# The sink columns of an attention kernel: four per head, turned by VectorE and gathered by DMAs, in place of eight turned by TensorE

## The chip, the cores and the metric

One core of one Trainium2 chip runs the whole kernel. The metric is device time in microseconds; the kernel before has a median of 690.72 us over three runs (690.72 to 690.74).

## The reference

Attention over a window of 128 keys and the first four keys ("sinks"), for 4 sequences of 768 positions and 8 heads of 64, and then two dense layers over all 3072 tokens:

```
scores = q k^T / 8,  kept where key < 4 or 0 <= query - key < 128
a = exp(scores - max) / (sum + 1e-9)
x = a v                       (3072 x 512, heads side by side)
out = relu(x w_in)^2 w_out    (512 -> 2048 -> 512)
```

All in float32, the weights given in float64.

## The kernel before, in words

The 3072 tokens are cut into eight chunks c of 384 (half a sequence), each with three blocks of 128 queries. For each chunk the attention runs in four steps s, one for a pair of heads; so there are 32 steps. Then come the first products (w_in, lines L778: twelve matmuls of 384 columns per piece of 128 hidden channels), the activation on ScalarE (L791, L795) and VectorE (L800, L807), which split the square into a high part gh and a low part gl, and the second products (L823: nine matmuls of 512 columns per piece). The products of chunk c cover the attention of chunk c + 1. Products go in two or three passes of rounded float32 ("fp32r": high and low parts).

One attention step: the scores of a block of 128 queries against 128 + NS + 128 columns (own and previous key block and NS sink columns: BAND = 264 with NS = 8) on TensorE (L483 in the first eight steps, "plain", with full float32; L489 with high and low parts after that); mask, scale and row maximum on VectorE (L466); exp on ScalarE (L472); sums and reciprocals on VectorE (L529, L530); scaling by 1/sum on GpSimd (L537), or on ScalarE (L535) in the plain steps. Then the probabilities P are turned, keys to partitions. In the first two chunks ("turned") TensorE transposes P (L638) and ScalarE copies to PT or PTS. From the third chunk on VectorE turns 32 x 32 blocks (L668, L672) into T, four DMAs store T in DRAM (via, L685) and one loads it as PT (L698).

The sink columns go another way. GpSimd copies those of both heads into PSK (L552) in three groups of 32 columns: a high part, a low part (L550) and the high part once more. TensorE transposes each block of PSK (L590), in all 32 steps: two 128 x 128 transposes in the first half of a sequence (its first block has no sink columns beside the window) and three in the second half. A copy takes the result from PSUM to SK (L600). The product with v (L726, two matmuls side by side on half the columns of the array) is closed by one matmul of SK with VS (L730), whose rows hold v at the sinks: high parts, high parts, low parts (L374, L379).

The order of each engine's instructions is written out by a planner (class Plan). Every step is added with an engine, or a list of engines to choose from, a cost, a rank, the cells that it reads and writes, and the PSUM banks that it takes and gives back. The planner goes through time with these costs: on each engine, of the steps that could start within 0.03 us of the first, it takes the one with the lowest rank. It knows that GpSimd and some VectorE steps ("port") hinder each other, that a change of TensorE's tiling costs something, and that a DMA takes its time and its share of the rate. The engines then run their lists strictly in order.

Of the kernel before, what the change touches and what calls it, by code (L numbers as in the profile page):

```python
# [19 lines left out]
D = 64  # L20
NS = 8
# [11 lines left out]
EPS = 1.0e-9  # L33
URGE = 0.5
# [15 lines left out]
class Plan:  # L50
# [45 lines left out]
    def order(self):  # L96
# [3 lines left out]
        while open_:  # L100
# [24 lines left out]
            if e == "PE":  # L125
                cost += 0.17 * (kind[0] != mode)
                mode = kind[0]
# [27 lines left out]
def sink_window_attention_moe(  # L155
# [25 lines left out]
    with ExitStack() as fast:  # L181
# [78 lines left out]
        SK = [sb("SK", [P, TOK], F32R, "SK_0"), sb("w22", [P, TOK], F32R, "SK_1")]  # L260
# [100 lines left out]

        def sinks(b, rank):
            rows = vs.shape[1]
            raw = lambda: sb("VR", [rows, NPAIR, P], F32, f"vs_{b}")
            lo = slice(64, 64 + 2 * NS)
# [5 lines left out]
                writes=["VR"],  # L371
# [3 lines left out]
                reads=["VR"], writes=["VS"],  # L375
# [3 lines left out]
                lambda: nc.vector.tensor_tensor(VS[lo], raw()[lo], f32(VS[lo]), op=ALU.subtract),  # L379
                reads=["VR"], writes=["VS"],  # L380
            )

        def attention(s, rank):
# [117 lines left out]
            for m, (i, heads) in enumerate(order):  # L501
# [3 lines left out]
                if plain:  # L505
                    reads, cost = [q_cell, (k_cell, 0), (k_cell, 1)], (0.44 if n > P else 0.23)
                else:
# [5 lines left out]
                    reads=reads, writes=keys, take=[("any" if early else "att", key) for key in keys],  # L513
# [27 lines left out]
            two = s % 2 if plain else 0  # L541
            psk = PSK[two]
            psk_cell = "PSK" if two == 0 else ("spare", 23)
            to = psk.rearrange("p q (t c) -> p q t c", c=32)

            def part_sinks(h, low):
                own = slice(h * NS, h * NS + NS)
                src = Pt(h)[:, i0:NQ, P:BS]
                if low:
                    nc.gpsimd.tensor_tensor(to[:, i0:NQ, 1, own], src, f32(to[:, i0:NQ, 0, own]), op=ALU.subtract)  # L550
                else:
                    nc.gpsimd.tensor_copy(  # L552
                        to[:, i0:NQ, 0:3:2, own], src.unsqueeze(2).broadcast_to([P, NQ - i0, 2, NS])
                    )

            groups = ((0, 1),) if plain else ((0,), (1,))
            for heads in groups:
# [6 lines left out]
                for h in heads:  # L564
                    for i in range(NQ):
# [3 lines left out]
                            [pool, ("ACT", 0.38 if n > P else 0.28, "", SC_ACT)] if plain else [pool, pool], r - URGE,  # L569
# [6 lines left out]
                        reads=done, writes=[(psk_cell, h)] + ([] if two == 0 else [psk_cell]),  # L576
# [6 lines left out]
            sk = SK[two]  # L583
            sk_cell = "SK" if two == 0 else ("spare", 22)
            nsq = (NQ - i0) * P
            key = ("sk", s)

            def turn_sinks():
                for i in range(i0, NQ):
                    nc.tensor.transpose(bank(key)[:, (i - i0) * P : (i - i0 + 1) * P], f32(psk[:, i]), ident)  # L590

            r = rank(0.95)
            add(
                ("PE", 0.11 * (NQ - i0), 0), r, turn_sinks,
                reads=[(psk_cell, h, *x) for h in range(2) for x in ((), (1,))] + ([] if two == 0 else [psk_cell]),
                writes=[key], take=[("any" if early else "att", key)],
            )
# [4 lines left out]
            on_act, on_dve = ("ACT", 0.36 if nsq == TOK else 0.3, "", 0.0), ("DVE", 0.48 if nsq == TOK else 0.36, "", CP_DVE)  # L602
            add(
# [556 lines left out]
```

## Time and profile before

| | |
|---|---|
| median of three runs | 690.72 us |
| the profiled execution | 688.96 us |
| its span, first to last instruction | 686.9 us |
| mean granted clock of TensorE | 0.991 |
| TensorE busy | 667.4 us (97%) |
| VectorE, ScalarE, GpSimd busy | 459.1, 375.0, 215.2 us |
| DMA queue of the kernel | 103.98 MB, 49.7% of 16 engines |

Lines such as L778 are lines of the kernel before. In a row, PE is TensorE, PEld its weight loads, DVE VectorE, ACT ScalarE, POOL GpSimd, SPq the queue of SyncE, which issues all DMAs. A row of a timeline gives the start, the time from the first start to the last end of the merged instructions, engine, line, operation, output and inputs, how many, and in brackets the idle time ahead and what ended it. Matmuls overlap, so the duration of one is longer than the time to the start of the next.

### The profile page before, as it was taken

To read this page: it belongs to the slowest core of one execution; us is meant where nothing else is said; L and a number is where in the kernel's file an instruction comes from. 1 tells how busy PE (TensorE), PEld (TensorE's weight loads), DVE (VectorE), ACT (ScalarE), POOL (GpSimd) and SP (SyncE) were. 2 spreads that over 40 slices of the span, in tenths; PEclk is the share of its full clock that TensorE was granted. 3 is DMA by queue.
4 is the path that set the end of the run, shared out by engine and by line. 5 is a ranking of instruction groups with operands and counts; after the bars stand their busy time and mean duration, and the time that the engine had idled before them with its cause. 6 is when DMAs were issued, how large, how long until landed. Compare 5 with 4: busy or idle time off the path is not lost.

```text
span 686.9 us, 11380 instructions
## 1 busy us (share of the span) xinstructions
PE 667.4 (97%) x3722; PEld 581.1 (85%) x3722; DVE 459.1 (67%) x1194; ACT 375.0 (55%) x1073; POOL 215.2 (31%) x377
## 2 busy tenths in 40 slices
PE   4999989999999999999999999999999999999996
PEld 3667879998888888888888898888898888899985
DVE  7599999967987655676677766666776764242222
ACT  6798734355464434456666656666666565442221
POOL 4455433534544513232244323223332322000000
PEclk9799999999999999999999999999999999999999
DMA  7746455215777532466556666555557754310001
GB/s 244 220 163 203 168 192 183 84 52 157 223 245 227 154 106 93 134 207 193 155 148 184 211 188 201 170 167 174 145 169 213 223 160 114 116 51 12 0 1 51
DMA packets 58178, 104.78 MB, mean 153 GB/s; under 512 B 6208, under 2 KB 34624, under 8 KB 58112
## 3 DMA queue, kind: packets, MB, share of 16 engines
q1 hardware_dynamic: 58112, 103.98, 49.7%
q8 instruction: 31, 0.51, 0.3%
q14 instruction: 35, 0.29, 0.1%
HBM read 79.58 MB, written 24.38 MB: 151 GB/s over the span
## 4 chain that ended last, share of the span: by engine, by line
PE 90%; DVE 6%; ACT 1%; issue 1%; DMA 1%; SPq 0%; POOL 0%; DVEq 0%
PE bank L823 37%; PE bank L778 37%; PE bank L726 6%; PE bank L489 5%; PE bank L730 1%; DVE f L310 1%; PE bank L590 1%; PE bank L483 1%; DVE P L466 1%; PE bank L638 1%; DVE f L317 1%; DVE f L303 1%; DMA kn<-in_k_dram 1%; ACT w L323 0%; DVE w L327 0%
## 5 line engine op out<-in xcount | busy, mean ns | idle before, releaser
L778 PE MATMUL bank<-x,w 128*128 128x384 f32 x1536 | 303.1, 339 | 0.7 <-DVE gl L807 0.7
L778 PEld LDWEIGHTS bank<-x,w 128*128 128x128 f32 x1536 | 267.0, 188 | 9.5 <-issue 1.4
L823 PE MATMUL bank<-w,gh 128*128 128x512 f32 x768 | 242.7, 397 | 2.1 <-ACT ob L864 2.1
L823 PEld LDWEIGHTS bank<-w,gh 128*128 128x128 f32 x768 | 137.5, 188 | 21.4 <-ACT ob L864 2.4
L823 PE MATMUL bank<-w,gl 128*128 128x512 f32 x384 | 151.4, 394 | 0.0
L446 POOL TENSOR_TENSOR KS<-kn,KS 128x408 fp32r<-128x408 f32 (+1 forms) x48 | 64.9, 1352 | 225.1 <-DVE KS L441 164.2
L791 ACT ACTIVATE r<-bank 128x384 f32<-128x384 f32 x128 | 62.7, 490 | 129.3 <-PE bank L778 128.2
L472 ACT ACTIVATE P<-P,nbs 128x264 f32<-128x264 f32 (+1 forms) x192 | 94.4, 492 | 66.5 <-DVE nbs L466 65.7
L800 DVE TENSOR_TENSOR bank<-bank,r 128x384 f32<-128x384 f32 x128 | 72.1, 563 | 83.4 <-ACT r L791 83.1
L537 POOL TENSOR_SCALAR P<-P,small 128x128 f32<-128x128 f32 (+1 forms) x168 | 88.5, 543 | 71.1 <-DVE small L530 48.9
L823 PEld LDWEIGHTS bank<-w,gl 128*128 128x128 f32 x384 | 72.1, 188 | 16.6
L466 DVE CUSTOM_DVE_ANT_0 P<-bank,maskA 128x264 f32<-128x264 f32 x128 | 53.4, 426 | 45.1 <-PE bank L489 43.6
L807 DVE TENSOR_TENSOR gl<-bank,gh 128x384 fp32r<-128x384 f32 x128 | 70.9, 554 | 17.4 <-ACT gh L795 11.8
L795 ACT ACTIVATE gh<-r 128x384 fp32r<-128x384 f32 x128 | 66.7, 521 | 4.7 <-PE bank L823 2.2
L668 DVE STREAM_TRANSPOSE T<-P 128x384 f32<-128x384 f32 x96 | 45.2, 495 | 22.6 <-POOL P L537 21.7
L489 PEld LDWEIGHTS bank<-KS,QS 128*128 128x128 f32 x288 | 51.6, 188 | 6.2 <-DVE nbs L466 0.4
L489 PE MATMUL bank<-KS,QS 128*128 128x264 f32 (+1 forms) x288 | 55.4, 279 | 0.0
L742 ACT CAST x<-bank 128x384 fp32r<-128x384 f32 x32 | 15.3, 478 | 52.6 <-PE bank L730 52.4
L327 POOL TENSOR_TENSOR w<-f,w 128x512 fp32r<-128x512 f32 x19 | 27.1, 1430 | 51.4 <-ACT w L323 51.4
L726 PE MATMUL bank<-PT,vn 128*64 128x256 f32 (+1 forms) x392 | 40.6, 347 | 0.0
L726 PEld LDWEIGHTS bank<-PT,vn 128*64 128x64 f32 x392 | 25.7, 139 | 15.5 <-issue 6.7
L529 DVE TENSOR_TENSOR small<-small,eps 128x3 f32<-128x3 f32 (+1 forms) x56 | 34.5, 616 | 3.3 <-ACT P L472 2.7
(90 smaller groups left out, 575.5 us busy)
## 6 DMA issues: line engine op xcount, KB each, us to landing
raw<-in_moe_w_dram SPq DMA_DIRECT2D x32, 512.0 KB, 3.7
half<-in_moe_w_dram SPq DMA_DIRECT2D x64, 256.0 KB, 3.6
via<-T SPq DMA_DIRECT2D x48, 192.0 KB, 3.7
PT<-via SPq DMA_DIRECT2D x12, 768.0 KB, 4.4
via<-T SPq DMA_DIRECT2D x48, 160.0 KB, 4.2
PT<-via SPq DMA_DIRECT2D x12, 640.0 KB, 4.7
kn<-in_k_dram SPq DMA_DIRECT2D x24, 272.0 KB, 4.4
qn<-in_q_dram SPq DMA_DIRECT2D x32, 192.0 KB, 3.6
```

The lines of the kernel that those rows point to most:

```text
L446: lambda h=h: nc.gpsimd.tensor_tensor(KS(h)[:, 1, 0:nk], kn()[:, h, 0:nk], f32(KS(h)[:, 0, 0:nk]), op=ALU.subtract),
L466: nc.vector.tensor_tensor_reduce(Pt(h)[:, i, o : o + n], ps_[:, 0:n], mask[:, 0:n], -SCALE, BIG, ALU.add, ALU.min, nb)
L472: nc.scalar.activation(Pt(h)[:, i, o : o + n], Pt(h)[:, i, o : o + n], AF.Exp, bias=nb, scale=-1.0, accum_out=sm[:, h, i : i + 1],)
L489: nc.tensor.matmul(bank(key)[:, 0:n], QS(h)[:, cols], flat[:, a, c0 : c0 + n], start=(a == 0), stop=(a == 1),)
L537: {"POOL": nc.gpsimd, "DVE": nc.vector}[engine].tensor_scalar(a, a, rs[:, h, i : i + 1], 1.0, op0=ALU.mult, op1=ALU.mult)
L726: nc.tensor.matmul(xo[h * D : h * D + D, qs[0] * P : qs[0] * P + len(qs) * P], vn[:, kk, h, :], rhs(), start=(n == 0), stop=False, skip_gr ...
L778: nc.tensor.matmul(bank(key)[:, 0:TOK], wi[fc][:, i, cc * P : (cc + 1) * P], xt[:, cc, :], start=(cc == 0 and j == 0), stop=(cc == NCC - 1 ...
L791: lambda key=key, r=r: nc.scalar.activation(r(), bank(key)[:, 0:TOK], AF.Relu),
L795: ("ACT", 0.41), n - 9, lambda gh=gh, r=r: nc.scalar.activation(gh(), r(), AF.Square),
L800: lambda key=key, r=r: nc.vector.tensor_tensor(bank(key)[:, 0:TOK], bank(key)[:, 0:TOK], r(), op=ALU.mult),
L807: lambda key=key, gh=gh, gl=gl: nc.vector.tensor_tensor(gl(), bank(key)[:, 0:TOK], f32(gh()), op=ALU.subtract),
L823: nc.tensor.matmul(bank(okey), gt()[:, ts_], wo[f][:, i, :], start=(f == f0 and j == 0), stop=(f == f1 - 1 and j == 2),)
```

## The change

NS becomes 4, so a score block has 260 columns. The rest of the change has three parts.

The turning of the sinks. In the steps from the third chunk on, PSK is 32 columns wide: 4 columns of two heads, three times (high, low, high), 24 in use. VectorE turns each 32 x 32 block (L633) into SKT, four DMAs gather the four strips of 32 partitions (L639) into a tile that shares its place with the raw rows of v at the sinks, and a copy (L610) on ScalarE or VectorE brings them into 32 partitions of SK. The closing product (L776) reads SK with a pattern (block, strip, 32 columns), and VS has its low parts in rows 16 to 23 (made with a column "third" of 0 and -1). The first eight steps keep the transposes on TensorE (L616), from a wide PSK that has two buffers.

The engines for scalings. In the eight plain steps VectorE may scale too (L556), beside GpSimd and ScalarE.

The planner. A GpSimd step and a "port" step of VectorE hinder each other for half their cost (SHARE) instead of all; a step that could start up to 0.15 us later (HOLD) but has a rank lower by more than 8 goes first; a tiling change costs 0.2 instead of 0.17 and is also counted at the end of a step; the scores of a later step are put in order only when the tile for P is free (CLAIM).

```
-NS = 8
+NS = 4
+SHARE = 0.5
+HOLD = 0.15
+SC_DVE = 0.3
+CLAIM = (True, False)
...
+                urgent = [x for x in able if x[0] <= first + HOLD and x[1] < a[1] - 8]
+                if urgent:
+                    a = min(urgent, key=lambda a: a[1:3])
...
-                    port[e] = t + cost
+                    port[e] = t + SHARE * cost
...
-        PSK = [sb("PSK", [P, NQ, P], F32R, "PSK_0"), sb("w23", [P, NQ, P], F32R, "PSK_1")]
-        for t in (VS, *PSK):
+        PSK = [wp.tile([P, NQ, 32], F32R, name=f"PSK{i}") for i in range(2)]
+        SKT = wp.tile([P, NQ, 32], F32, name="SKT")
+        SK = [sb("SK", [P, 4, NQ, 32], F32R, "SK_0"), sb("w22", [P, 4, NQ, 32], F32R, "SK_1")]
+        PSKW = sb("w23", [P, 2, NQ, P], F32R, "PSK_wide")
+        for t in (VS, PSKW, *PSK, *SK):
             nc.gpsimd.memset(f32(t), 0.0)
...
-                    reads=reads, writes=keys, take=[("any" if early else "att", key) for key in keys],
+                    reads=reads + [P_cell(h) for h in heads] * (CLAIM[plain] and i > 0),
+                    writes=keys + [P_cell(h) for h in heads] * (CLAIM[plain] and i == 0), take=[...],
...
-                            [pool, ("ACT", 0.38 if n > P else 0.28, "", SC_ACT)] if plain else [pool, pool], r - URGE,
+                            [
+                                pool, ("ACT", 0.38 if n > P else 0.28, "", SC_ACT),
+                                ("DVE", 0.25 if n > P else 0.18, "port", SC_DVE),
+                            ] if plain else [pool, pool], r - URGE,
...
+            else:
+                add(
+                    ("DVE", 0.18), rank(1.0) - URGE,
+                    lambda: nc.vector.transpose(SKT[:, i0:NQ], f32(psk[:, i0:NQ])), reads=own_sinks, writes=["SKT"],
+                )
+                rows_ = lambda: sb("VR", [P, 4, NQ, 32], F32, f"sk_{s}")
+                def gather(x):
+                    nc.sync.dma_start(
+                        out=rows_()[0:32, x, i0:NQ].rearrange("p i b -> p (i b)"),
+                        in_=SKT[32 * x : 32 * x + 32, i0:NQ].rearrange("p i b -> p (i b)"),
+                    )
+                for x in range(4):
+                    add(
+                        ("SP", 0.42, 2.5, 13), rank(0.85), lambda x=x: gather(x), reads=["SKT"], writes=[("VR", x)],
+                    )
+                add(
+                    [("ACT", 0.4), ("DVE", 0.35, "port", CP_DVE)], rank(0.8) - URGE,
+                    lambda e: copy(e, sk[0:32, :, i0:NQ], rows_()[0:32, :, i0:NQ]),
+                    reads=VR, writes=[sk_cell],
+                )
...
-                    xo[:, i0 * P : TOK], VS[:, p], sk[:, 0:nsq], start=False, stop=True, skip_group_check=True
+                    xo[:, i0 * P : TOK], VS[:, p], sk[:, :, i0:NQ].rearrange("p r i b -> p i r b"), start=False, stop=True, skip_group_check=True
```

How the order moves, at three places. First TensorE in the third quarter of the program, in a step of a second half: the product with v closes, and the transposes of the next step's sinks follow. Before:

```order
L726 MATMUL bank_67<-PT,vn_136 64x256 x4
L726 MATMUL bank_67<-PT,vn_136 64x128 x4
L730 MATMUL bank_67<-SK_132,VS 128x384
L778 MATMUL bank_71<-x_140,w_996 128x384 x2
L778 MATMUL bank_71<-x_141,w_996 128x384
L590 MATMUL bank_69<-ident,PSK_127 128x128 x3
L823 MATMUL bank_74<-w_971,gh_597 128x512 x2
L823 MATMUL bank_74<-w_971,gl_605 128x512
```

And after:

```order
L772 MATMUL bank_69<-PT,vn_146 64x256 x4
L772 MATMUL bank_69<-PT,vn_146 64x128 x4
L776 MATMUL bank_69<-SK_130,VS 128x384
L824 MATMUL bank_70<-x_150,w_987 128x384 x2
L824 MATMUL bank_70<-x_151,w_987 128x384
L869 MATMUL bank_74<-w_959,gh_597 128x512 x2
L869 MATMUL bank_74<-w_959,gl_606 128x512
```

The three transposes between first and second products are gone, and nothing stands in their place; the same holds for two or three of them in 24 steps.

Second VectorE in such a step. Before, the copy of the transposes of the sinks (SK) stands right behind the turning of P (T), between the product and the subtraction of the activation:

```order
L668 STREAM_TRANSPOSE T_3764<-P_1_3746 128x2x4x32
L672 STREAM_TRANSPOSE T_3764<-P_1_3746 128x4x32
L747 TENSOR_TENSOR x_139<-bank_68,x_138 128x384
L800 TENSOR_TENSOR bank_71<-bank_71,r_567 128x384
L864 COPY ob_0_0_3872<-bank_74 128x512
L807 TENSOR_TENSOR gl_590<-bank_71,gh_578 128x384
L600 CAST SK_132<-bank_67 128x384
```

And after, where SKT is VectorE's turning of the sinks and sk the tile that the four DMAs fill:

```order
L633 STREAM_TRANSPOSE SKT<-PSK_128 128x96
L718 STREAM_TRANSPOSE T_3822<-P_1_3801 128x4x32
L793 TENSOR_TENSOR x_149<-bank_68,x_148 128x384
L846 TENSOR_TENSOR bank_70<-bank_70,r_560 128x384
L853 TENSOR_TENSOR gl_586<-bank_70,gh_579 128x384
L910 COPY ob_0_0_3934<-bank_72 128x512
L910 COPY ob_0_2_3943<-bank_73 128x512
...
L610 CAST SK_130<-sk_3908 32x384
```

The copy of the sinks now stands one step of the products behind the turning, and ahead of the next product (L846); the two reductions of scores ahead of it are left out. On SP the four gathers stand behind a load of v and ahead of most of the stores of T in such a step.

Third the first scalings of the program, on GpSimd. Before (P_0_171 and P_1_173 are the two heads of the first step):

```order
L537 TENSOR_SCALAR P_0_171<-P_0_171,small 128x128
L537 TENSOR_SCALAR P_0_171<-P_0_171,small 128x264 x2
L537 TENSOR_SCALAR P_1_173<-P_1_173,small 128x128
L537 TENSOR_SCALAR P_1_173<-P_1_173,small 128x264 x2
L552 CAST PSK_127<-P_0_171 128x4x8
```

And after:

```order
L556 TENSOR_SCALAR P_0_181<-P_0_181,small 128x128
L556 TENSOR_SCALAR P_0_181<-P_0_181,small 128x260
L556 TENSOR_SCALAR P_1_187<-P_1_187,small 128x260
L572 CAST PSK_wide<-P_0_181 128x2x2x4
L572 CAST PSK_wide<-P_1_187 128x2x2x4
```

The other three of the six now stand on VectorE, between its reductions of the scores. In all, VectorE has 16 scalings in the first eight steps, ScalarE 7 instead of 24, and GpSimd's number is one higher.

More of the change, by code (lines that the diff above doesn't have):

```diff
@@ L378, in sinks @@
                 ("DVE", 0.62, "port"), rank,
-                lambda: nc.vector.tensor_tensor(VS[lo], raw()[lo], f32(VS[lo]), op=ALU.subtract),
-                reads=["VR"], writes=["VS"],
+                lambda: nc.vector.scalar_tensor_tensor(
+                    VS[0:rows], f32(VS[0:rows]), third[0:rows], raw(), op0=ALU.mult, op1=ALU.add
+                ),
+                reads=VR, writes=["VS"],
             )
@@ L581, in attention @@
                     )
-            sk = SK[two]
-            sk_cell = "SK" if two == 0 else ("spare", 22)
-            nsq = (NQ - i0) * P
+            sk_cell = ("spare", 22) if two and plain else "SK"
+            sk = SK[1 if two and plain else 0]
             key = ("sk", s)
[L588 to L597, printed above, removed]
+            own_sinks = [(psk_cell, h, *x) for h in range(2) for x in ((), (1,))]
@@ L599, in copy, with turn_sinks @@
             def copy(engine, dst, src):
                 nc.scalar.copy(dst, src) if engine == "ACT" else nc.vector.tensor_copy(dst, src)
-            on_act, on_dve = ("ACT", 0.36 if nsq == TOK else 0.3, "", 0.0), ("DVE", 0.48 if nsq == TOK else 0.36, "", CP_DVE)
-            add(
-                [on_act, on_dve] if plain else [on_dve, on_dve], r - URGE,
-                lambda e: copy(e, sk[:, 0:nsq], bank(key)[:, 0:nsq]), reads=[key], writes=[sk_cell], drop=[key],
-            )
+            if turned:
+                def turn_sinks():
+                    for i in range(i0, NQ):
+                        nc.tensor.transpose(bank(key)[:, i * P : (i + 1) * P], f32(psk[:, i]), ident)
+                r = rank(0.95)
+                add(
+                    ("PE", 0.11 * (NQ - i0), 0), r, turn_sinks, reads=own_sinks + [("spare", 23)], writes=[key], take=[("any" if early else "att", key)],
+                )
+                add(
+                    [("ACT", 0.3, "", 0.0), ("DVE", 0.36, "", CP_DVE)], r - URGE,
+                    lambda e: copy(
+                        e, sk[0:32, :, i0:NQ],
+                        bank(key)[0:32, i0 * P : TOK].rearrange("p (i r b) -> p r i b", r=4, b=32),
+                    ),
+                    reads=[key], writes=[sk_cell], drop=[key],
+                )
[11 more added lines that the diff above has]
+                for x in range(4):
+                    add(
+                        ("SP", 0.42, 2.5, 13), rank(0.85), lambda x=x: gather(x), reads=["SKT"], writes=[("VR", x)],
+                    )
+                add(
+                    [("ACT", 0.4), ("DVE", 0.35, "port", CP_DVE)], rank(0.8) - URGE,
+                    lambda e: copy(e, sk[0:32, :, i0:NQ], rows_()[0:32, :, i0:NQ]),
+                    reads=VR, writes=[sk_cell],
+                )
```

42 lines of the change are left out of this document (23 added, 19 removed).

## The prediction

> **What bounds the kernel now.** I read the page's busy shares first, then the stretches of the span, then the matmuls themselves in order of time, and last the waits. The page, and six stretches (each row: the stretch, its length, busy time of TensorE, weight loads, VectorE, ScalarE and GpSimd with their counts, granted clock, DMA share, GB/s):
>
> ```profile
> PE 667.4 (97%) x3722; PEld 581.1 (85%) x3722; DVE 459.1 (67%) x1194; ACT 375.0 (55%) x1073; POOL 215.2 (31%) x377
> 15.00:20.00 5.00, 2.37 (x10) 1.45 (x9) 4.00 (x11) 3.64 (x11) 5.00 (x9) 0.57 1.00 292
> 20.00:25.00 5.00, 5.00 (x24) 3.12 (x24) 1.32 (x8) 3.54 (x12) 3.45 (x13) 0.50 0.77 258
> 25.00:30.00 5.00, 5.00 (x38) 3.69 (x36) 3.33 (x10) 3.82 (x11) 0.00 (x0) 0.91 0.54 171
> 60.00:95.00 35.00, 35.00 (x214) 29.60 (x213) 33.84 (x61) 24.27 (x56) 15.77 (x19) 1.00 0.53 182
> 95.00:100.00 5.00, 2.89 (x16) 2.45 (x16) 4.94 (x8) 1.95 (x4) 1.49 (x2) 1.00 0.37 133
> 230.00:600.00 370.00, 370.00 (x2084) 326.88 (x2083) 236.66 (x618) 213.17 (x647) 112.37 (x206) 1.00 0.56 165
> ```
>
> TensorE is the bound of the whole (97%). From 230 to 600 it is never idle, so there only its own work counts: an instruction taken from it is time gained, one put on VectorE (236.66 of 370) or ScalarE (213.17) is hidden. From 60 to 95 VectorE has 33.84 of 35 and TensorE 35 of 35: there a load moved to VectorE is not hidden for sure. TensorE has a hole at 15 to 20 and one at 95 to 100, and a granted clock of about one half for 10 us (0.43/0.5 of 5, all of 5, 0.09/0.5 of 5: 4.3 + 5 + 0.9).
>
> **The change part by part.** First, the transposes of the sinks on TensorE (L590) fall from 80 to 20. What one costs is not its duration, since matmuls overlap, but what it adds from start to start. Matmuls of a pair of the later chunks, with two transposes, and of another with three:
>
> ```profile
> L590 PE MATMUL bank<-ident,PSK 128*128 128x128 f32 x80 | 14.3, 278 | 0.0
> 335.58 0.62 PE L823 MATMUL bank<-w,gh 128*128 128x512 f32 x2
> 336.04 0.39 PE L823 MATMUL bank<-w,gl 128*128 128x512 f32 x1
> 336.27 0.38 PE L590 MATMUL bank<-ident,PSK 128*128 128x128 f32 x2
> ...
> 336.94 0.39 PE L823 MATMUL bank<-w,gl 128*128 128x512 f32 x1
> ...
> 356.23 0.49 PE L590 MATMUL bank<-ident,PSK 128*128 128x128 f32 x3
> ...
> 357.03 0.40 PE L823 MATMUL bank<-w,gl 128*128 128x512 f32 x1
> ```
>
> Two gh products alone take 336.04 - 335.58 = 0.46 to the next start; with two transposes ahead 336.94 - 336.27 = 0.67, with three 357.03 - 356.23 = 0.80. So two cost 0.21 and three 0.34. Of the 24 pairs that lose them 12 have two (first half of a sequence) and 12 three: 12 x 0.21 + 12 x 0.34 = 6.6. All 24 lie after 100 us, where TensorE is full: -6.6.
>
> Second, the scores get 260 columns instead of 264. By the rows above a product of 512 columns takes 0.46 / 2 = 0.23, so 0.45 ns a column, and 240 matmuls of four columns less give 0.43; the 20 early score pairs at a like rate add 0.1 to 0.2. If short instructions have a floor it is nothing. I take -0.5, with 0 as the other end.
>
> Third, what TensorE keeps. The sinks product (now L776) reads its moving side in pieces of 32 columns; no row of before has that for SK, but the products with P read PT in such pieces in the later chunks and PTS in one piece in the early ones. Their twelve take 354.78 - 353.54 = 1.24 in pieces and 30.36 - 29.12 = 1.24 in one:
>
> ```profile
> 29.12 1.30 PE L726 MATMUL bank<-PTS,vn 128*64 128x128 f32 x12
> 30.36 0.39 PE L730 MATMUL bank<-SK,VS 128*128 128x256 f32 x1
> 353.54 1.30 PE L726 MATMUL bank<-PT,vn 128*64 128x256 f32 x12
> 354.78 0.39 PE L730 MATMUL bank<-SK,VS 128*128 128x256 f32 x1
> ```
>
> So pieces cost nothing. The number of tiling changes in TensorE's order falls by one or two; nothing.
>
> Fourth, what the turning costs elsewhere: 24 transposes on VectorE (0.27 for the nearest row, one of 128 columns; these have 64 or 96), 96 more issues on SP, and 24 copies of 32 rows, 10 on VectorE and 14 on ScalarE, for 24 on VectorE out of PSUM:
>
> ```profile
> L672 DVE STREAM_TRANSPOSE T<-P 128x128 f32<-128x128 f32 x24 | 6.6, 274 | 0.0
> L600 DVE CAST SK<-bank x24: 406/486/558, 154.1 to 579.1; 128x256 fp32r<-128x256 f32 x12, 128x384 fp32r<-128x384 f32 x12
> 316.83 0.41 DVE L600 CAST SK<-bank 128x256 fp32r<-128x256 f32 x1
> 334.82 0.39 PE L730 MATMUL bank<-SK,VS 128*128 128x256 f32 x1
> 315.46 2.07 SPq L685 DMA_DIRECT2D via<-T  x4
> via<-T SPq DMA_DIRECT2D x48, 192.0 KB, 3.7
> pari<-in_params_dram SPq DMA_DIRECT2D x1, 2.0 KB, 2.6
> 321.89 0.56 SPq L698 DMA_DIRECT2D PT<-via  x1
> PT<-via SPq DMA_DIRECT2D x12, 640.0 KB, 4.7
> ```
>
> VectorE loses 24 x 0.486 = 11.7 and gets at most 24 x 0.27 + 10 x 0.56 = 12.1: even, and hidden under TensorE's 370 of 370; with that cover gone it costs 0.4. ScalarE's 14 copies, up to 0.56 each, are 7.8 more in 500 us and hidden likewise. A gather of 8 or 12 KB has no row; it lands between 2.6 (2 KB) and 3.7 us (192 KB) after its issue, and four issues take 2.07 us like those of via. So the sinks stand in SBUF 4.2 to 5.3 us after VectorE's transpose (1.6 to the fourth issue). In VectorE's new order the copy stands one product step or more behind the transpose; a step is nine products of 512 columns and twelve of 384 on TensorE, at 0.46/2 = 0.23 for 512 some 2.1 us each, 4.2 together, and scores between. The product with VS itself has room: its SK was copied at 316.83 for 334.82, 18 us ahead. I take the wait as hidden, with the other end as rival (c). On SP the issues stand ahead of the stores of T, so these go 2.07 later: the product with P has room for it, as its load PT, issued at 321.89 and landing in about 4.7, is there 7 us ahead of it (1.24 before 334.82).
>
> Fifth, the first 100 us. Sixteen of the scalings by 1/sum go to VectorE and 17 leave ScalarE; GpSimd's first six shrink to three. What TensorE waited for there, and the price of a scaling on VectorE (nearest: 0.29 for 256 columns):
>
> ```profile
> 12.39 5.21 POOL L537 TENSOR_SCALAR P<-P,small 128x128 f32<-128x128 f32 x6 [5.66 <-DVE small L530]
> 17.65 0.69 PE L638 MATMUL bank<-ident,P 128*128 128x128 f32 x2 [2.47 <-POOL P L537]
> L233 DVE TENSOR_SCALAR ge<-rel 128x256 f32<-128x256 f32 x1 | 0.3, 288 | 0.0
> 98.02 0.62 ACT L323 CAST w<-f 128x512 fp32r<-128x512 f32 x1 [3.92 <-DVE f L317]
> 99.20 0.71 PE L823 MATMUL bank<-w,gh 128*128 128x512 f32 x2 [2.11 <-ACT ob L864]
> ```
>
> Best end: three scalings on GpSimd end by 12.4 + 2.6 (half of 5.21) instead of 17.6, so the transposes start 2.6 sooner; that stretch runs at clock 0.5, so it is worth 1.3; and the 2.11 at 99.2 goes, because ScalarE's copy ob no longer stands right behind a cast (98.02) that waits for late weights. Together -3.4. Worst end: 16 x 0.29 = 4.6 of new VectorE work ahead of the copies of ob at 98.4 with none of it hidden: +4.6. Against that VectorE had 1.00 + 3.68 + 1.67 = 6.4 of idle time from 15 to 30. That cover is larger than the load, so I choose near the good end but not at it, because from 60 to 95 TensorE can run ahead only as far as VectorE's 33.84 of 35 lets it, and what it gains comes back as a longer wait at 99: -1.0. The new clears on GpSimd and the column third stand ahead of GpSimd's idle 5.66 in the first row, and cost nothing; two small VectorE instructions of under 0.2 stand beside the first score stage. What comes after the last attention step holds nothing that the change touches.
>
> How VectorE and GpSimd go together in that part, these rows show:
>
> ```profile
> 67.45 0.42 DVE L303 TENSOR_SCALAR f<-raw 128x512 int32<-128x512 int32 x1
> 92.17 2.92 POOL L327 TENSOR_TENSOR w<-f,w 128x512 fp32r<-128x512 f32 x2 [2.81 <-ACT w L323]
> 92.43 1.52 DVE L303 TENSOR_SCALAR f<-raw 128x512 int32<-128x512 int32 x1
> ```
>
> The same VectorE instruction takes 0.42 alone and 1.52 beside GpSimd's subtraction of 92.17; and GpSimd's first six scalings took 0.87 each (5.21). The Trainium skill (SBUF — State Buffer, "Who interferes with whom") has the port pair of VectorE and GpSimd as an exclusive lock, whose loser blocks for the whole instruction. By that rule the split scalings run one after another and hold up the other engine, and the time would be that of rival (b). The 1.52 agrees with a full block; that the same instruction takes 0.42 at 67.45 says that it strikes only where GpSimd is at work.
>
> The sum: the profiled span is 686.9, the profiled run 688.96, the median of the runs 690.72, so 3.8 lie around the span. 686.9 - 6.6 - 0.5 - 1.0 = 678.8, and 678.8 + 3.8 = 682.6.
>
> **The rivals.** (a) The early part gains more: with no hole ahead of the first transposes the clock isn't halved. TensorE's work from 15.7 to 25.9 (2.37 + 5.00 + 0.9, at half speed) would be half as long: 4 us more, 678.6. For it: the hole ahead of 17.65 is the reason nearest to the low clock. Against it: the new order still leaves TensorE without work between the last scores and the first transposes, some 2 us. The Trainium skill (TensorE: Matmul & The Clock Gate, Part 1) has the clock fall to one half after an idle window of about 3.4 us and stay until a busy one; the 10.2 us at one half fit three such windows.
>
> (b) The early part loses: VectorE's 4.6 isn't hidden and delays the copies of ob: 690.7 - 7.1 + 4.6 = 688.2. It decides once VectorE's idle time of 6.4 is no longer there to take the 4.6. For it: 33.84 busy of 35 from 60 on, and 4.94 of 5 at the hole; against it: the idle time lies just where the scalings go.
>
> (c) Slower: a gather lands after its copy is due. The copy stands in order ahead of the product by r (L800, now L846) or of the square (L795, now L841); behind it hang gl and the second product, and TensorE's room there has run out once already, as the first of these rows of waits shows; the second is SP's wait with loads of v, behind which the gathers stand:
>
> ```profile
> PE bank L778 <- DVE gl L807: 0.7, 1, 0.7
> SPq L417 <- PE bank L730: 20.9, 22, 4.1
> ```
>
> Of a late gather between nothing and all reaches TensorE. v's wait is 1 us on average; with 1 us late and half of it reaching TensorE, 24 pairs cost 12: 690.7 - 7.1 + 12 = 695.6. The loss outweighs the gain of 7.1 from 0.3 us a pair on. Against it: one step of 4.2 and more between transpose and copy.
>
> (d) It does nothing: TensorE's freed time is taken by waits that were hidden behind the transposes: 690.5. Against it: 370.00 busy of 370.
>
> **How the numbers follow.** My forecast, 682.6 (its own range 680 to 685.5, from the fifth term between -3.4 and +2 and the second at 0), has 0.64; (a) 0.12, (b) 0.11, (c) 0.09, (d) 0.04. The range goes from 678, which takes (a) in, to 689, which takes (b) in; (c) and (d), 0.13, are left out. A measurement of this kernel tells about 0.2%, 1.4 us, from no change. Faster by more than that are forecast, (a) and (b): 0.87; the same (d): 0.04; slower (c): 0.09.
>
> **What would show it.** L616 has 20 transposes and none after 100 us; the stretch from 230 to the last attention holds TensorE without idle time and is about 5 us shorter for the same products; the first product with P starts before 23.26; the wait for ob near 97 is below or about 2. It is wrong if TensorE's idle time names the copies L610, their gathers, or gl L853, over and over, or if the wait for ob grows by more than the start gained.

## The result, and the profile after

The changed kernel takes 682.8 us (682.0 to 683.5), the kernel before 690.7: a ratio of 0.9888, 95% interval 0.9871 to 0.9906. The profiled execution's span is 679.8, its time 682.0. The forecast was 682.6.

The busy line of the changed kernel's page, its stretches (columns as in the prediction), the group of the transposes that are left, and what TensorE waited for (us in total, times, longest):

```profile
PE 659.6 (97%) x3662; PEld 573.2 (84%) x3662; DVE 460.5 (68%) x1221; ACT 374.1 (55%) x1070; POOL 211.9 (31%) x383
```

```profile
15.00:20.00 5.00, 2.87 (x22) 1.76 (x20) 4.93 (x14) 3.95 (x13) 3.02 (x5) 1.00 1.07 279
20.00:25.00 5.00, 4.74 (x39) 3.36 (x37) 4.59 (x14) 4.57 (x13) 5.00 (x12) 1.00 1.04 264
60.00:95.00 35.00, 32.68 (x191) 27.52 (x190) 33.65 (x64) 20.72 (x45) 15.04 (x16) 1.00 0.56 175
95.00:100.00 5.00, 5.00 (x29) 4.74 (x28) 4.87 (x10) 1.80 (x4) 2.15 (x2) 1.00 0.79 280
230.00:600.00 370.00, 370.00 (x2064) 326.06 (x2063) 235.26 (x634) 220.00 (x669) 108.31 (x206) 1.00 0.57 168
```

```profile
L616 PE MATMUL bank<-ident,PSK_wide 128*128 128x128 f32 x20 | 3.8, 287 | 3.1 <-POOL PSK_wide L570 3.1
```

```profile
PE bank L616 <- POOL PSK_wide L570: 3.1, 2, 2.3
PE bank L684 <- POOL P L556: 2.4, 4, 1.2
PE bank L772 <- DMA PT<-via: 0.9, 1, 0.9
PE bank L824 <- DVE gl L853: 0.6, 1, 0.6
PE bank L869 <- DVE ob L910: 0.5, 1, 0.5
```

L616 has 20 transposes, all in the first 100 us. From 230 to 600 TensorE is as full as before, and its 2064 matmuls for 2084 hold no transposes of sinks. The wait of 2.1 for ob at 97 has gone, and one of 2.3 for GpSimd has come at 72. To see where time went I set the start of the same matmul in both traces side by side. The mark is the first of the second products of the 21st hidden step, called O20 here (at 151.64 in the kernel before). Every pair of heads whose sinks TensorE no longer turns comes behind it (the first transpose of these at 153.26), and from there TensorE waits once, for 0.7 us, in the kernel before, and once, for 0.9 us (PT at 203), in this trace of the changed one. Two executions of the kernel before agree to 0.01 us from O20 to TensorE's last matmul (529.31 and 529.30), so a difference there is the kernel's own.

O20 is thus the border between the start of the program and its steady part. All runs, with the median of each and, of its one profiled execution, the time to O20, from O20 to TensorE's last matmul, from there to the end of the span, and the time at half clock ahead of O20 (all in us):

```
                                     median  ratio [95%]              to O20  to last  to end  half clock
before (in four groups of runs) 690.3-690.9  -                        151.64  529.31   5.9     10.2
  again                                      -                        153.31  529.30   5.9     13.7
changed                              682.83  0.9888 [0.9871, 0.9906]  150.52  522.54   6.8      0
  again                              682.81  0.9885 [0.9870, 0.9900]  151.01  522.28   6.9      3.4
four sinks alone                     689.49  0.9984 [0.9972, 0.9997]  151.74  529.46   6.2     10.2
changed, sinks turned by TensorE     689.05  0.9977 [0.9965, 0.9988]  151.43  529.59   7.2      3.4
turning and four sinks alone         683.49  0.9894 [0.9879, 0.9909]  151.47  521.83   6.9      6.8
  with VectorE's scalings too        681.80  0.9869 [0.9853, 0.9885]  151.50  522.18   7.0     10.2
changed, no scaling on VectorE       685.94  0.9928 [0.9915, 0.9942]  154.79  522.34   7.0      6.8
changed, gathers by two hops         681.76  0.9871 [0.9855, 0.9886]  151.37  521.62   6.9      3.4
changed, weights 32 bytes on         684.62  0.9910 [0.9896, 0.9925]  151.71  523.68   7.1      3.4
changed, gh and gl 32 bytes on       684.29  0.9907 [0.9893, 0.9922]  153.32  521.75   7.2      6.8
changed, more scalings on ScalarE    684.95  0.9915 [0.9896, 0.9934]  152.15  522.61   7.4      3.4
  and both of 32 bytes               685.95  0.9930 [0.9912, 0.9949]  150.70  522.22   7.3      0
```

So the gain of the two first profiles, 7.0, is 1.1 ahead of O20, 6.8 behind it, and 0.9 lost behind the last matmul.

### The profile page after: what moved, and what is told of

It reads as the page before. It is cut to its first block, busy times and chain, and to the rows that moved or that the text cites. A ratio compares the mean times of both kernels' runs of the same rounds, so it can differ in the third digit from the quotient of the medians.

```text
span 679.8 us, 11460 instructions
## 1 busy us (share of the span) xinstructions
PE 659.6 (97%) x3662; PEld 573.2 (84%) x3662; DVE 460.5 (68%) x1221; ACT 374.1 (55%) x1070; POOL 211.9 (31%) x383
## 4 chain that ended last, share of the span: by engine, by line
PE 84%; DVE 10%; ACT 2%; DMA 2%; issue 1%; POOL 1%; SPq 0%; DVEq 0%; ACTq 0%
PE bank L869 36%; PE bank L824 35%; PE bank L772 5%; PE bank L507 5%; DVE f L332 2%; DVE f L325 2%; PE bank L776 1%; PE bank L501 1%; DMA PT<-via 1%; DVE P L484 1%; DVE f L318 1%; DVE bank L846 1%; DVE w L342 1%; DVE gl L853 1%; PE bank L684 1%
## 5 line engine op out<-in xcount | busy, mean ns | idle before, releaser
L464 POOL TENSOR_TENSOR KS<-kn,KS 128x396 fp32r<-128x396 f32 (+1 forms) x48 | 65.0, 1355 | 238.4 <-DVE KS L459 200.8
L846 DVE TENSOR_TENSOR bank<-bank,r 128x384 f32<-128x384 f32 x128 | 71.9, 562 | 81.0 <-ACT r L837 80.6
L490 ACT ACTIVATE P<-P,nbs 128x260 f32<-128x260 f32 (+1 forms) x192 | 93.7, 488 | 58.5 <-DVE nbs L484 57.3
L556 POOL TENSOR_SCALAR P<-P,small 128x260 f32<-128x260 f32 (+1 forms) x169 | 84.6, 516 | 63.7 <-DVE small L549 47.4
L484 DVE CUSTOM_DVE_ANT_0 P<-bank,maskA 128x260 f32<-128x260 f32 x128 | 52.7, 419 | 46.5 <-PE bank L507 46.1
L507 PE MATMUL bank<-KS,QS 128*128 128x260 f32 (+1 forms) x288 | 55.1, 277 | 0.0
L342 POOL TENSOR_TENSOR w<-f,w 128x512 fp32r<-128x512 f32 x20 | 29.6, 1481 | 44.5 <-ACT w L338 38.6
L548 DVE TENSOR_TENSOR small<-small,eps 128x3 f32<-128x3 f32 (+1 forms) x56 | 37.1, 662 | 2.9 <-ACT P L490 2.1
```

The costliest lines, as they stand in the source:

```text
L464: lambda h=h: nc.gpsimd.tensor_tensor(KS(h)[:, 1, 0:nk], kn()[:, h, 0:nk], f32(KS(h)[:, 0, 0:nk]), op=ALU.subtract),
L484: nc.vector.tensor_tensor_reduce(Pt(h)[:, i, o : o + n], ps_[:, 0:n], mask[:, 0:n], -SCALE, BIG, ALU.add, ALU.min, nb)
L490: nc.scalar.activation(Pt(h)[:, i, o : o + n], Pt(h)[:, i, o : o + n], AF.Exp, bias=nb, scale=-1.0, accum_out=sm[:, h, i : i + 1],)
L507: nc.tensor.matmul(bank(key)[:, 0:n], QS(h)[:, cols], flat[:, a, c0 : c0 + n], start=(a == 0), stop=(a == 1),)
L556: {"POOL": nc.gpsimd, "DVE": nc.vector}[engine].tensor_scalar(a, a, rs[:, h, i : i + 1], 1.0, op0=ALU.mult, op1=ALU.mult)
L846: lambda key=key, r=r: nc.vector.tensor_tensor(bank(key)[:, 0:TOK], bank(key)[:, 0:TOK], r(), op=ALU.mult),
```

## The experiments

**Both kernels again.** Nothing edited.

> The changed kernel once more, nothing edited: how far does it repeat itself? Two things of the first profile are in question. (1) Its second products (L869, 512 columns) stood 232.7 ns apart in the last leg, against 230.3 before. If that belongs to the kernel (its order or the places of its buffers), it shows 232 to 233 again; if it varies from execution to execution, it lies anywhere from 230 to 233, and the time varies with it by up to 2 us. (2) The granted clock was 1.00 all through the first 30 us. If the shorter start keeps it up for good, it is 1.00 again; if it stands on an edge, as the mean clocks of its other runs (0.994 and 0.996 against 0.998) suggest, a stretch at one half comes back, of 3 to 5 us. Time 681.5 to 684.

> The kernel before once more, nothing edited. Its eleven runs here lie between 689.25 and 691.43, and the first profile (span 686.9) lies at the fast end, so that the time gained between the two first profiles (7.1) is less than that between the medians (8.1). If the places of the buffers set the spacing of the matmuls, the spacings of the last leg repeat: second products 231.3 ns (changed kernel 233.4, twice), first products 175.4 (changed kernel 174.3, twice); and what made this execution of another length lies in the first 30 us and behind the last matmul. If the spacing varies from execution to execution, it is another. Span 687 to 689.5.

The two expectations give spacings of second products that differ by 0.7 to 1 ns for the same traces (232.7 and 233.4, 230.3 and 231.3), which changes no comparison; below, those of the second are used.

The changed kernel repeats itself behind O20 to 0.26 us. Ahead of it, the clock differs: a stretch of 3.4 us at half speed is back (0.08 / 0.5 x 5 + 0.26 / 0.5 x 5). Its stretches:

```profile
15.00:20.00 5.00, 3.20 (x21) 2.08 (x21) 4.93 (x15) 3.63 (x12) 2.79 (x7) 0.92 1.02 300
20.00:25.00 5.00, 5.00 (x35) 4.15 (x35) 3.65 (x12) 3.98 (x12) 4.32 (x11) 0.74 0.99 291
```

The second trace of the kernel before shows what its first profile (span 686.9), which was faster than its usual runs, did not have. Its stretch from 100 to 105, and the second product that waited for ob:

```profile
100.00:105.00 5.00, 5.00 (x20) 4.59 (x19) 4.41 (x9) 0.56 (x2) 0.00 (x0) 0.66 0.48 174
```

```profile
99.38 0.70 PE L823 MATMUL bank<-w,gh 128*128 128x512 f32 x2 [2.14 <-ACT ob L864]
```

Behind the hole of 2.14 the clock is halved for 3.4 us (0.34 / 0.5 x 5), which the first profile did not have after its hole of 2.11. That is most of the difference, and not in the first 30 us, where the expectation looked for it: the same matmuls start 0.13 to 0.17 us later from 26 to 94 us (0.18 at the product of 99.38), 1.67 later from 117 us on, and it stays so. So this half clock costs 1.5. The mean clock of eleven runs of the kernel before is 0.987 to 0.991, seven of them at 0.989 like this one and two at 0.991 like the first profile; so most runs probably have one half clock more than the profile that the forecast was made from. That does not explain all of the first profile's lead: nine runs at 0.991 on record took 689.3 to 690.8, and it took 688.96.

**The turning undone.**

```diff
-            if turned:
+            if True:        # sinks by TensorE and a copy out of PSUM in all chunks
                 def turn_sinks():
```

> Of the change, only the turning is undone: in the later chunks too the sinks are turned by TensorE, two or three transposes of 128 x 128 a pair, out of a buffer 128 columns wide, and copied out of PSUM; no gathers. Four sinks per head, the planner's settings and the scalings on VectorE stay. My theory, that the steady gain is the transposes taken from TensorE: 60 transposes come back, 12 x 0.21 + 12 x 0.34 = 6.6 by the forecast's price, 5.0 to 5.6 by the gain seen between the two profiles; so the time is 687.8 to 689.5, slower than the changed kernel by 5 to 6.6, and the start (first product with P near 16.3) is unchanged. Rival, that the new order and settings gave the gain and the transposes' time is taken by something else: within 1.5 of the changed kernel. Second question: if the second products stand 232 to 233 ns apart here too, the wider spacing does not come from the gathers.

It takes 689.05, 6.2 more than the changed kernel, and 529.59 behind O20 for 522.28: 7.3. Its groups show the transposes come back:

```profile
L613 PE MATMUL bank<-ident,PSK_late 128*128 128x128 f32 x60 | 10.6, 274 | 0.0
L613 PE MATMUL bank<-ident,PSK_wide 128*128 128x128 f32 x20 | 3.9, 297 | 3.0 <-POOL PSK_wide L567 3.0
```

So the gain in the steady part is the turning, and new order and settings give none of it there (529.59 against 529.30 of before).

**Four sinks alone.**

```diff
-NS = 8
+NS = 4
```

> The kernel before with four sinks per head in place of eight and nothing else: scores of 260 columns for 264, the transposes of the sinks still on TensorE. By the forecast it is worth 0.5; by the runs so far 1.85 go to all but the turning together, and 0.7 of that to settings and VectorE's scalings, so up to 1.2: 689.7 to 690.4, start as before. The smaller tiles of k and P also move the weights in SBUF by 32 bytes against the first products' x (from 32 past a multiple of 64 to a multiple); if the places of the buffers set the spacing of the second products (231.3 ns in the last leg of the kernel before, 233.4 in that of the changed kernel), it is another here; if not, it is 231.3. Rival: below what is measured, 690.5 to 691.3.

The median falls by 1.0 (ratio 0.9984, interval 0.9972 to 0.9997), but behind O20 nothing is gained (529.46 for 529.31). Summing there by kind the times from each matmul's start to the next one's: attention's matmuls take 75.05 for 75.39, so the columns are worth 0.34; the first products 225.39 for 226.19; the second products 228.62 for 227.33. The last two have the same shapes as before; what is known to be different is where their operands lie, which moves such spacings (below). In the changed kernel the same sum gives the products 225.49 and 227.31, no more than before, and attention 69.34; so what a kind gets depends on what stands next to it, and only the sums of whole runs are sure. The 1.0 of the median thus comes from outside that stretch, probably ahead of O20, where the executions differ by half clocks: its seven runs with a mean clock of 0.991 or 0.992 took 687.3 to 689.6, its five with 0.989 or 0.990 took 690.6 to 691.5.

**Turning and four sinks alone, then with VectorE's scalings, and the changed kernel without these.**

```diff
-SHARE = 0.5
-HOLD = 0.15
-CLAIM = (True, False)
+SHARE, HOLD, CLAIM = 1.0, -1.0, (False, False)   # and tiling change 0.17, old prices
-                                ("DVE", 0.25 if n > P else 0.18, "port", SC_DVE),
```

> The turning by VectorE with its gathers and the four sinks per head alone: the planner has its old settings (no claims, no hold, full port lock, the tiling change at 0.17), and no scaling may go to VectorE. My theory, that the steady gain needs only the turning and the early gain only the rest: the stretch from O12 to O112 is as short as in the changed kernel, the start is as before (first product with P near 23, half clock for some 10 us), so it is 2 to 3.5 us slower than the changed kernel, 685 to 686.5. Rival, that the planner's settings are what keeps the gathers hidden: waits for the copies of SK, or for PT, on TensorE, and no faster than 688.

> Turning, four sinks and scalings on VectorE, but the planner with its old settings (no claims, no hold, full port lock, tiling change 0.17). It fills the square: old settings without VectorE's scalings 683.5, new settings without them 685.9, new settings with them 682.8. Theory, that the new settings are worse than the old ones by themselves and the scalings are what pays: 681 to 682.8. Rival, that settings and scalings only pay together (the half port lock is what lets the planner put scalings on VectorE beside GpSimd): 683.3 to 685.

> The changed kernel without the choice of VectorE for a scaling: the first pair's six scalings stand on GpSimd one after the other again, all else stays. My theory, that the split of the first six scalings brings the early gain, by a shorter hole and by a clock that is not halved: the first product with P goes back to 20 to 23 us, the clock shows about one half for about 10 us, and the time is 684.5 to 686.5. Rival, that the early gain comes from the order (claims and hold): the hole and the half clock come back but the first product of the second leg's outputs still starts 2 us or more sooner than in the kernel before (99.2), and the time stays within 1 us of the changed kernel.

Old settings without and with VectorE's scalings: 683.5 and 681.8; new settings: 685.9 and 682.8. VectorE's scalings are worth 3.1 with the new settings. With the old ones the medians differ by 1.7, but the intervals overlap and the two traces are level at O20 (151.47 and 151.50), so a gain there is not shown. The new settings lose 2.4 without the scalings, and with them 1.0, which the intervals don't tell from nothing. Behind O20 the three lie within 0.5 us of each other: settings and scalings act in the first 150 us alone. Of the expectations, the one for the turning alone named the steady part rightly, but the start was to cost 2 to 3.5 us against the changed kernel and costs 0.7: its first product with P is late (22.72) as expected and its clock at half for 6.8 us instead of some 10, yet at O20 it is 0.5 to 1 us behind. The waits of TensorE without VectorE's scalings and with the new settings:

```profile
PE bank L683 <- POOL P L556: 3.3, 6, 0.9
PE bank L615 <- POOL PSK_wide L570: 2.0, 5, 0.7
PE bank L868 <- DVE gl L852: 1.3, 1, 1.3
PE bank L868 <- DVE ob L909: 1.1, 1, 1.1
```

Many small waits for GpSimd, and it arrives at O20 3.2 us behind the first trace of the kernel before and 1.5 behind the second. Its time is as expected, and the rival, that order alone brings the early gain, falls by it. But the mechanism of the expectation was wrong too: the first product with P was to go back to 20 to 23 us and the clock to one half for about 10. It starts at 18.06, and the half clock lasts 6.8. With VectorE's scalings and the old settings it starts at 24.48, later than in the kernel before (23.26). The row without VectorE's scalings, and the row with them and the old settings:

```profile
18.06 2.40 PE L771 MATMUL bank<-PT,vn 128*64 128x128 f32 x12
```

```profile
24.48 2.39 PE L772 MATMUL bank<-PT,vn 128*64 128x128 f32 x12
```

So the early first product comes mostly from the new settings (22.72 to 18.06 without VectorE's scalings, 24.48 to 16.27 with them), and that VectorE takes some of the first scalings is not enough for it. What VectorE's scalings are worth lies further on.

**A longer way for the gathers.** Four DMAs to DRAM and one back, in place of four within SBUF.

```diff
-                        out=rows_()[0:32, x, i0:NQ].rearrange("p i b -> p (i b)"),
+                        out=hop()[:, x, i0:NQ].rearrange("p i b -> p (i b)"),
                         in_=SKT[32 * x : 32 * x + 32, i0:NQ].rearrange("p i b -> p (i b)"),
...
+                        out=rows_()[0:32, :, i0:NQ].rearrange("p r i b -> p r (i b)"),
+                        in_=hop()[:, :, i0:NQ].rearrange("p r i b -> p r (i b)"),
```

> The changed kernel with a longer way for the sinks: VectorE's turned tile goes by four DMAs to DRAM and from there by one DMA to SBUF, in place of four DMAs from SBUF to SBUF; one landing of some 3 us and a fifth issue on SP more for each of the 24 pairs. My theory, that the gathers have room: in the changed kernel SK stands ready 8 to 13 us ahead of the product with P, so 3 to 4 us later costs nothing: 682 to 683.5. Rival (c) of the forecast, that the copy behind the gather holds up ScalarE and so gl and the second product: 24 pairs lose some 0.3 us or more each, 690 or more, with waits for the copy of SK or for gl on TensorE.

681.8: no slower. The landings in the changed kernel and, in the second fence, in this one (KB each, median us from issue to landing):

```profile
sk<-SKT SPq DMA_DIRECT2D x48, 8.0 KB, 2.6
sk<-SKT SPq DMA_DIRECT2D x48, 12.0 KB, 2.2
```

```profile
hop<-SKT SPq DMA_DIRECT2D x48, 8.0 KB, 3.0
hop<-SKT SPq DMA_DIRECT2D x48, 12.0 KB, 2.6
sk<-hop SPq DMA_DIRECT2D x12, 48.0 KB, 3.3
sk<-hop SPq DMA_DIRECT2D x12, 32.0 KB, 2.5
```

One landing more, of 2.5 to 3.3, and no wait on TensorE: rival (c) was at least that far away. In the changed kernel ScalarE's copies do wait for gathers now and then (3.1 us over 5 times, by the rows of waits), and none of it reaches TensorE.

**Where the operands lie.** The changed kernel's new tile of four bytes (third) takes 32 bytes ahead of everything else in SBUF, and the smaller tiles of k and P shift what lies behind them; so x came to a multiple of 64 bytes, and gh and gl too, with almost all of the weights w 32 past one. Before, x, gh, gl and almost all of w lay 32 past. Two kernels in the changed kernel's order, with unused tiles of 32 bytes:

```diff
         nc.gpsimd.memset(eps, EPS)
+        wp.tile([P, 8], F32, name="pad0")    # second kernel: gh, gl and all behind
...
+        wp.tile([P, 8], F32, name="pad1")    # second kernel, ahead of x; the first has one, behind x
```

> The changed kernel with an unused tile of 32 bytes behind x: q, k, P, T and the weights w lie 32 bytes further on, so the weights at a multiple of 64; gh, gl and x stay at a multiple of 64, and the order of all work is the same. Theory of places: where the second products' two operands lie sets their spacing; in the kernel before gh and w both lie 32 past a multiple of 64 (231.3 ns in the last leg), in the changed one gh at a multiple and w 32 past (233.4); here both lie at a multiple. If what counts is that they lie alike, it goes to 231.3 or below and the time falls by 2 to 2.5 us, to 680.5; if what counts is gh alone, 233.4 stays. Rival, that places don't matter and the order does: 233.4 and 682.8.

> The changed kernel with an unused tile of 32 bytes ahead of gl and gh and another ahead of x: gh and gl lie 32 past a multiple of 64 as in the kernel before, x at a multiple and the weights 32 past as in the changed one; the order of all work is the same. Theory of places: the second products go back to 231.3 ns and the time falls by 2 to 2.5 us, to 680.5, with the first products at 174.3. Rival, that places don't matter: 233.4 and 682.8.

Both expectations of a gain were wrong: 684.6 and 684.3. But places do matter: the order of work on every engine is the same as in the changed kernel, and the spacings are not. The mean time from start to start in the last leg, where nothing else is done (130 to 210 of each per trace): first products 175.4 before, twice; 174.3 in all seven traces with the places of the changed kernel; 175.6 with the weights moved; 173.5 with gh and gl moved, twice. In every one of these kernels in which x and w lie alike to 64 bytes it is 175.4 or more, in every one in which they differ by 32 it is 174.3 or less; why is open. The second products go 231.3 before, twice; 233.3 to 233.4 in the seven; 232.4 and 232.5 with the turning undone and with four sinks alone; 233.7 and 234.4 here: they repeat as well, but by no rule that I found. From O20 on, against the second trace of the changed kernel, the weights moved cost 1.4 us, and gh and gl moved gain 0.5; the latter loses 2.3 ahead of O20, where in its trace the clock is halved behind the hole at 74:

```profile
76.68 0.90 PE L618 MATMUL bank<-ident,PSK_wide 128*128 128x128 f32 x3 [2.33 <-POOL PSK_wide L572]
```

```profile
75.00:80.00 5.00, 3.32 (x14) 3.22 (x15) 3.98 (x7) 1.51 (x3) 2.42 (x6) 0.66 0.54 171
```

**A try at the hole at 72.** In the changed kernel GpSimd holds up TensorE there, with VectorE at work beside it all the time:

```profile
70.11 3.29 POOL L556 TENSOR_SCALAR P<-P,small 128x260 f32<-128x260 f32 x4 [1.02 <-DVE small L549]
73.36 1.26 POOL L572 CAST PSK_wide<-P 128x24 fp32r<-128x24 f32 x2
75.02 0.55 PE L616 MATMUL bank<-ident,PSK_wide 128*128 128x128 f32 x3 [2.32 <-POOL PSK_wide L570]
```

```diff
-SC_ACT = 0.3
+SC_ACT = 0.1
-                        pool = ("POOL", 0.46 if n > P else 0.33)
+                        pool = ("POOL", (0.8 if n > P else 0.55) if plain else (0.46 if n > P else 0.33))
```

> A try to go past the changed kernel. In it TensorE waits 2.3 us from 72.7 on for GpSimd, which takes 3.29 us for four scalings and 1.26 for two casts while VectorE has the port, and ScalarE has 20.7 of 35 us busy there. Here the planner prices GpSimd's scalings of the early chunks at 0.8 and 0.55 as the trace has them (for 0.46 and 0.33) and ScalarE's handicap is 0.1 for 0.3, so that more of them go to ScalarE (24 for 7) and fewer to GpSimd and VectorE. Theory, that the hole at 72 is GpSimd's and comes out of the end: hole gone, 680.5 to 682. Rival, that VectorE's work on the weights (33.65 of 35 us from 60 to 95) sets when TensorE passes 100 us: the hole moves to waits for gl, ob or the weights near 95 to 120, and the time is 682.5 to 684.

> The one before with the two unused tiles of 32 bytes again (ahead of gl and gh, and ahead of x). With them in the changed kernel the first products stood 173.5 ns apart for 174.3 and the second ones 234.4 for 233.4, the stretch from O32 to O108 was 0.4 us shorter and the start lost 2.5 us to half clocks behind the holes at 15 and 72. If the places set the spacings, they are 173.5 and 234.4 again, with another order of the early work; and if the loss came from the holes, it is gone with the one at 72: 680 to 682. Rival: the tiles cost time by themselves, 1.5 us more than the kernel without them.

The hole goes, and the time rises to 685.0 and 686.0. Its stretch from 60 to 95, and what TensorE waits for:

```profile
60.00:95.00 35.00, 34.50 (x208) 29.00 (x203) 34.36 (x68) 22.28 (x52) 14.85 (x19) 1.00 0.61 198
```

```profile
PE bank L684 <- ACT P L554: 2.3, 2, 1.5
PE bank L824 <- DVE x L793: 1.3, 1, 1.3
PE bank L684 <- DVE P L556: 1.1, 1, 1.1
PE bank L869 <- DVE ob L910: 1.1, 1, 1.1
```

TensorE's idle time from its first to its last matmul is 10.1 us for 8.9 in the changed kernel: the hole's 2.3 has come back as smaller waits for VectorE and ScalarE, as the rival had it, though 685.0 is above what the rival gave too (682.5 to 684), and 686.0 is outside the 680 to 682 of the second. The second kernel's six runs lie from 682.1 to 687.1, and their mean clocks (0.998 the fastest, 0.997 the next, 0.989 to 0.991 the other four) go with that spread. Neither is a better version. Gathers by two hops, and the old settings with VectorE's scalings, have medians 1.0 below the changed kernel's, but the intervals overlap.

## Why the prediction came out right

**First (-6.6) and second (-0.5), the steady part: right in sum, each term off.** Behind O20 the changed kernel is 6.8 to 7.0 shorter for a forecast of 7.1. The turning carries all of it, and more than its price: undoing it costs 7.1 to 7.3, and with the old settings it gains 7.6 (529.46 with four sinks alone, 521.83 with the turning too). All the rest of the change together, forecast at -0.5, is +0.3 there (529.59 with the turning undone, for 529.31). The columns give their 0.34 in the attention's matmuls, but with four sinks alone the first and second products take 0.49 more; that this comes from the places of their operands is not shown. So the first term was 0.5 to 1.0 too small, the second had the wrong sign, and that they cancel to within 0.3 is luck.

**Third and fourth: right.** The sinks product, now read in pieces, takes 223 and 282 ns from its start to the next (256 and 384 columns), for 223 and 280 before. The turning's new work, and VectorE's scalings for the fifth term, in the groups of the changed kernel:

```profile
L633 DVE STREAM_TRANSPOSE SKT<-PSK 128x64 f32<-128x64 f32 (+1 forms) x24 | 5.5, 230 | 0.0
L610 DVE CAST SK<-sk 32x256 fp32r<-32x256 f32 (+1 forms) x10 | 3.0, 302 | 0.4 <-DMA sk<-SKT 0.2
L610 ACT CAST SK<-sk 32x384 fp32r<-32x384 f32 (+1 forms) x14 | 6.5, 462 | 3.8 <-DMA sk<-SKT 3.1 <-PE bank L776 0.7
L556 DVE TENSOR_SCALAR P<-P,small 128x260 f32<-128x260 f32 (+1 forms) x16 | 6.7, 462 | 0.0
```

VectorE takes 5.5 + 3.0 for 12.1 forecast at the most, ScalarE 6.5 for 7.8; the gathers land in 2.2 to 2.6, and two hops show room for one landing more. Behind O20 TensorE waits once in each trace of the changed kernel, 0.9 us for PT in one and 0.5 for a row sum (small) in the other, at 203 us. Rivals (c) and (d) fall.

**Fifth (-1.0): near in size, wrong in its working.** At O20 the changed kernel is 0.6 to 1.1 ahead of the first profile of before, 2.3 to 2.8 ahead of the second. That -1.0 was met is luck. The bounds were put together from the hole at 17 and the wait for ob. Both holes shrank as the good end had it: the wait is gone, and the first product with P starts at 16.27 in place of 23.26, as these rows of before and of the changed kernel show. But the split of the scalings, by which the forecast had the transposes start sooner, doesn't bring that by itself (24.48 with the old settings, above), and the wait for ob is gone with the turning and four sinks alone as well, where no scaling is on VectorE.

```profile
23.26 2.40 PE L726 MATMUL bank<-PT,vn 128*64 128x128 f32 x12
```

```profile
16.27 1.30 PE L772 MATMUL bank<-PT,vn 128*64 128x128 f32 x12
```

But in their place came a hole at 72, where the forecast looked for one near 97 only: TensorE's idle time from its first to its last matmul is 8.96 before and 8.93 after. In the two first traces, the same first product in count is 3.0 ahead at 70 us, 0.5 behind that hole at 88, 2.9 at 100 where before waits for ob, and 1.3 at 144; what takes the last 1.6 back is not shown. VectorE's scalings took 6.7 us for the 4.6 forecast, without rival (b)'s loss: with no scaling on VectorE the kernel is 3.1 slower. Of rival (a) its mechanism came and its price did not: the clock wasn't halved at all in the first profile, but a stretch at half clock there costs little. The two traces of the changed kernel differ by 3.4 us of it, 0.5 at O20 and 0.2 at the last matmul.

**Not in the forecast: the end, +0.9.** From the last matmul to the end of the span it takes 6.8 in place of 5.9. It was to hold nothing that the change touches; yet every kernel made from the changed one shows 6.8 to 7.4, with the turning undone too, and those made from the one before 5.9 to 6.2. In the trace the time passes behind SP's branch to the end of the program (from there to the end of the span 4.57 us for 3.33). What that waits for stays open.

**"3.8 lie around the span": wrong.** In the runs 1.7 to 2.2 lie around it (2.1 in the two first profiles). The rest is that the profiled execution of before was 1.8 below the median, most of it probably because it did not have the half clock behind the wait for ob. In spans the forecast was 678.8, and the runs of the changed kernel have 679.8 to 681.3. So the 682.6 holds two errors that cancel: the span was taken 1.0 to 2.5 too short (the end, and the half clock that most executions still have), what lies around it 1.7 too long. Against an execution of before like the second trace, the wait for ob was worth not 2.1 but 3.6, with the 1.5 of its half clock. That the median came out within 0.3 of the forecast is luck to that extent.

## What to carry to other kernels

Price an instruction on a full engine by what it adds from start to start, and count it only in the stretch where the engine never waits: the transposes so priced came to 6.6, and taking them out was worth 7.1 to 7.6. The term from a stretch with holes was put together from waits that the next wait replaced. Before summing against one profile, see whether it is a usual execution: compare its time and mean clock with the other runs, and look for holes after which the clock may or may not fall.

## What was not expected of the hardware

Half clock comes in pieces of 3.41 us: 0, 3.4, 6.8, 10.2 or 13.7 us in the fourteen traces. The Trainium skill (TensorE: Matmul & The Clock Gate, Part 1) tells of a window of 3413 ns that runs freely, which these lengths agree with. That same page has the clock fall after an idle window of about 3.4 us; here holes of 1.93 to 2.33 us were enough at 97 in two of three traces of kernels with that wait, and at 72 to 74 in one of six, so the trace differs there. Which of these nine holes it was goes by where they lay: all changes of the clock in one trace lie whole multiples of 3.413 us apart, which gives each trace a grid of windows. In the three that were followed by a half clock, 1.93, 1.97 and 2.14 us of the hole fell into one window; in the other six the border of a window cut it, and at most 1.72 fell into one. Nine holes are few, and in the first 30 us windows with 1.4 to 1.6 us of idle time were followed by a half clock too. What one piece costs goes by what TensorE has to do: 1.5 where it is full of products (100 to 104), while of one at 19 to 23, where it waits for others anyway, 0.5 is left behind between the two executions of the changed kernel.

And where operands lie in SBUF moves the spacing of the same matmuls by up to 2 ns of 175 and 3 ns of 232, the same in each execution: 32 bytes ahead of the weights cost this kernel 1.4 us over the 2243 such matmuls behind O20. Which place is good was not found: both tries at it ended slower.
